# Linear attention and two MLPs on one core: query buffers, the place of an output split, and how the next pass's weights and first operands are fetched

## The chip, the core and the metric

The program runs on one NeuronCore of one Trainium2 chip. The core has a matrix engine (TensorE, shown as PE, with its weight loads as PEld), a vector engine (VectorE, DVE), an activation engine (ScalarE, ACT), a general engine (GpSimd, POOL) and a sequencer that here issues nearly all DMAs (SyncE, SP). Each engine executes its own instructions strictly in the order in which the program lists them, and waits at an instruction until the semaphores that it needs are set. The metric is the device time of one execution in microseconds (us); lower is better.

## What is computed

The reference, cut to what matters:

```python
kv  = np.einsum('bhsd,bhse->bhde', k, v)           # 8 batches, 8 heads, 576 tokens, 64 wide
o   = np.einsum('bhsd,bhde->bhse', q, kv)
rms = np.sqrt(np.mean(o * o, axis=-1, keepdims=True) + 1e-06)
x   = o / rms * g_norm                              # as 4608 tokens x 512
h   = x @ w_in                                      # 512 x 2048
x   = np.maximum(0.01 * h, h) @ w_out               # 2048 x 512
h   = np.maximum(x @ w_in2, 0.0)                    # the second MLP
out = (h * h) @ w_out2
```

## The kernel before

All products are made in pairs of reduced-width float32 operands: a value is split into a high part (ACT copies it, rounding) and a low part (the difference), and a product is three matmuls, high by high, high by low, low by high.

**Pass 1** makes x and the first product, h = x @ w_in, block by block: 9 blocks of 512 tokens, and in each block 16 slots (block j, slot m), a slot being 12 matmuls of 512 columns in `gemm1` (line 471). `leaky` (line 483, on ACT) takes the sum out of PSUM into one of four buffers `h`, and SP stores it to a scratch tensor `g` in DRAM. Of the eight PSUM banks, `gemm1` uses four in turn. The attention that makes block j+1's x is spread over block j's slots, in 8 units of 256 tokens by 2 heads; block 0's own attention stands ahead of everything ("attention 0"). A unit goes through these stages: `stage_a` transposes q (line 368) and splits it into `qh` (ACT) and `ql` (DVE); `stage_b` makes the output `ops` (lines 384 to 386), its square `sq` and its copy `osb` (ACT), and splits the square into `sqh` (DVE, line 394) and `sql` (POOL, line 395); `stage_s` sums over the head (`ssps`, lines 401 and 402); `stage_c` makes the norm (`y`, `z` on ACT at lines 410 and 411, three DVE instructions at lines 412, 415 and 418, the last of which writes `osb`); `stage_d` splits `osb` into `xh` (ACT, line 427) and `xl` (POOL, line 428). The sixteen pieces of w_in are rounded by `scale_w` (ACT line 173, DVE lines 174 and 177) and `join_w` (DVE lines 187 and 191) and split by `split_w` (ACT line 203, POOL line 204), three of them in attention 0 and the rest in block 0. From block 1 on the weights of the later passes are rounded, summed and split the same way, and their operands stored to DRAM as `w2_01`, `w2_10` and `w2_11`.

**Pass 2** (line 662, with `ph` 0) multiplies `g` by w_out in seven products per two-by-two group instead of eight: a group is 7 steps of 12 matmuls of 256 columns. Its weight operands are 28 slots `w2_01_0` to `w2_01_27` of 512 KB, loaded by `fetch` (line 281); its data operands are loaded from `g` by `load_g2` (line 515, two loads of 512 KB for a group), summed on DVE (`sum_op`, line 542) and split on ACT (`hi_op`, line 557) and DVE (`lo_op`, line 562). Passes 3 and 4 do the same for the second MLP.

**What sets the order.** The list `prog` is written out by small tables: stages are put at slots, and sorted inside one slot by the tuple `order`. Nothing reorders it later; each engine's order is that of the list. Loads of q, k, v and raw weights stand as early in SP's order as there are free buffers: a load of q is emitted when `stage_a` frees one of the `Q_BUFS` buffers, and waits on SP until PE has read that buffer. Large SBUF tiles come from 42 slots; `take_big` hands out the one that has been free longest. `fetch` loads the next wanted weight slot when the number of resident weights is under `cap`; in pass 1's last block `gemm1` gives back one of the 16 w_in pieces after each slot and calls `fetch` again. A store of `h` is emitted one slot after its `leaky`.

Of the kernel before, what the change touches and what calls it, by code (L numbers as in the profile page):

```python
# [18 lines left out]
def tile_linear_attention_two_mlps(  # L19
# [36 lines left out]
    NM = DFF // P  # L56
# [7 lines left out]
    EPS = 1e-6  # L64
    LD_BUFS, Q_BUFS, KV_BUFS = 8, 3, 6

# [643 lines left out]
    with tc.manual_schedule():  # L710
# [9 lines left out]
        for u in sorted(steps):  # L720
            order = ("d", "b", "a", "s", "c", "kv", "gn", "scale", "join", "w")
            prog += sorted(steps[u], key=lambda st: order.index(st[0]))
        prog.append(("mlp",))
        slots = [(j, m) for j in range(NB) for m in range(NM)]
        steps = {}

# [26 lines left out]
        for s, (j, m) in enumerate(slots):  # L753
            if m == 0 and j + 1 < NB:
                at0, pace = (s - 4, 2) if j else (s, 1.4)
                put(at0, "x", j + 1)
                lags = (2, 4, 5) if j else (1, 2, 3)
                for n, sts in attention_steps(j + 1, pace, 0, *lags).items():
                    for st in sts:
                        put(at0 + n, *st)  # L760
        put(NM * (NB - 1), "cap", 28)
        put(NM * (NB - 1), "want", (0, 1), 0, NSLOT)
        late = ("w", "join", "scale", "ws", "w2")
        for s in range(len(slots)):
            st = steps.pop(s, ())
            prog += [x for x in st if x[0] in late]
            if s:
                prog.append(("lk", *slots[s - 1]))
            prog.append(("g1", *slots[s]))
            order = ("d", "s", "c", "b", "a", "kv")  # L770
            prog += sorted((x for x in st if x[0] in order), key=lambda x: order.index(x[0]))
            prog += [x for x in st if x[0] not in order and x[0] not in late]
        prog.append(("lk", *slots[-1]))
        assert not steps


        ev = []
# [41 lines left out]
        for x, (half, z) in enumerate(insts):  # L819
# [5 lines left out]
            if not (x and insts[x - 1][1] == z):  # L825
                lead = 11 if x and len(SETS[insts[x - 1][1]]) == 1 else 15
                at_slot(t0 - lead - XLEAD, "xl", z)
                for y, (kind, name) in enumerate(prep("T")):
# [36 lines left out]
        second_pass(t3, 1, [j for half, z in insts if half for j in SETS[z]])  # L865
        prog += [st for t, st in sorted(ev, key=lambda e: e[0])]
        prog += [("tick",)] * 3
# [84 lines left out]
```

## Time and profile before

| | |
|---|---|
| median of 3 runs | 1698.28 us (1698.13 to 1699.26) |
| profiled execution, device time | 1698.46 us |
| span shown by its profile | 1696.6 us |
| TensorE busy, VectorE busy, ScalarE busy | 95%, 72%, 47% of the span |
| mean granted TensorE clock over the span | 0.984 |

The profiled execution is 0.18 us over the median of the timed runs, and its span is 1.9 us shorter than its device time. Times inside the profile count from the start of the span. Pass 1 runs from 0 to 588 us, pass 2 from 598 to about 960 us. In a timeline row the columns are the start in us, the duration in us, engine, line, operation, output<-inputs, shapes and count; the square bracket gives how long the engine stood idle before the row and what ended the wait.

### The profile page before, as it was taken

What the parts mean: (1) busy time and instruction counts of PE and PEld (TensorE: products, weight loads), DVE (VectorE), ACT (ScalarE), POOL (GpSimd) and SP (SyncE); (2) the same over time, 40 slices, a digit from 0 to 9 for tenths busy, and PEclk for the clock granted to TensorE, in tenths of its full rate; (3) what the DMA queues carried; (4) which work ended last, traced back from release to release, by engine and by line L of the source; (5) the groups of instructions that cost most, each with busy time, mean ns of one, the idle gap of its engine ahead of it and who ended that gap; (6) DMA issues with size and microseconds to landing.
All of it is one profiled execution on the core that took longest, in us unless ns stands there. A gap on an engine that the chain in (4) does not pass through costs nothing. (4 is left out here: it accounts for less than half of the span.)

```text
span 1696.6 us, 28822 instructions
## 1 busy us (share of the span) xinstructions
PE 1613.3 (95%) x10672; PEld 1453.6 (86%) x10672; DVE 1227.0 (72%) x2047; ACT 792.8 (47%) x1655; POOL 269.4 (16%) x344
## 2 busy tenths in 40 slices
PE   5889989989989789999999999999999899999999
PEld 3668778778877589999999988878887899999999
DVE  5876677767675078888787787756876588788886
ACT  4656657566665144343444444434544344444342
POOL 3444455454545000000000000000000000000000
PEclk9999999999999989999999999999999999999999
DMA  7757979989976934444444744485457944334342
GB/s 192 218 153 222 319 239 313 290 276 305 316 271 238 407 137 128 128 132 132 146 134 149 280 149 156 161 286 173 149 167 261 346 140 140 128 125 131 125 135 84
DMA packets 249452, 338.50 MB, mean 200 GB/s; under 512 B 55264, under 2 KB 180192, under 8 KB 249312
## 3 DMA queue, kind: packets, MB, share of 16 engines
q1 hardware_dynamic: 249152, 336.67, 60.4%
q8 instruction: 84, 1.38, 0.3%
q14 instruction: 56, 0.46, 0.1%
q10 hardware_dynamic: 160, 0.00, 0.0%
HBM read 198.18 MB, written 138.41 MB: 198 GB/s over the span
## 5 line engine op out<-in xcount | busy, mean ns | idle before, releaser
L471 PE MATMUL hps<-xh,w 128*128 128x512 f32 x1152 | 388.0, 407 | 15.7 <-ACT xh L427 9.1
L471 PEld LDWEIGHTS hps<-xh,w 128*128 128x128 f32 x1152 | 222.6, 194 | 69.0 <-ACT xh L427 12.5
L471 PE MATMUL hps<-xl,w 128*128 128x512 f32 x576 | 231.4, 402 | 10.0 <-POOL xl L428 10.0
L471 PEld LDWEIGHTS hps<-xl,w 128*128 128x128 f32 x576 | 112.0, 195 | 33.9 <-POOL xl L428 13.3
L483 ACT ACTIVATE h<-hps 128x512 f32<-128x512 f32 x144 | 85.2, 592 | 47.2 <-DMA g<-h 36.5
L577 DVE TENSOR_TENSOR h_C<-aps,u 128x512 f32<-128x512 f32 x72 | 49.5, 688 | 64.4 <-PE aps L598 32.5
L412 DVE SCALAR_TENSOR_TENSOR z<-ssps,z 128x256 f32<-128x256 f32 x72 | 30.3, 421 | 86.5 <-ACT z L411 86.1
L395 POOL TENSOR_TENSOR sql<-sq,sqh 128x256 fp32r<-128x256 f32 x72 | 53.3, 741 | 204.5 <-DVE sqh L394 185.8
L428 POOL TENSOR_TENSOR xl<-osb,xh 128x256 fp32r<-128x256 f32 x72 | 63.6, 883 | 18.3 <-ACT xh L427 18.2
L577 DVE TENSOR_TENSOR u<-bps,p 128x512 f32<-128x512 f32 x72 | 49.4, 687 | 20.9 <-PE bps L598 10.8
L191 DVE SCALAR_TENSOR_TENSOR wt<-wt,w_raw 128x512 uint32<-128x512 uint32 x64 | 58.7, 917 | 2.2
L174 DVE TENSOR_SCALAR w_raw<-w_raw 128x512 uint32<-128x512 uint32 x64 | 36.3, 567 | 30.0 <-ACT wt L173 29.9
L410 ACT ACTIVATE y<-ssps,eps 128x256 f32<-128x256 f32 x72 | 33.9, 471 | 51.4 <-PE ssps L402 51.2
L615 ACT ACTIVATE h_C<-aps 128x512 f32<-128x512 f32 x36 | 21.5, 598 | 77.1 <-issue 30.0
L598 PE MATMUL aps<-op_B21h,w 128*128 128x512 f32 (+1 forms) x160 | 52.2, 375 | 5.3 <-ACT p L608 5.3
L177 DVE SCALAR_TENSOR_TENSOR w_raw<-w_raw 128x512 uint32<-128x512 uint32 x64 | 55.6, 869 | 2.2
L598 PE MATMUL aps<-op_B22h,w 128*128 128x512 f32 (+1 forms) x160 | 52.0, 375 | 2.5 <-DVE h_C L577 2.5
L598 PE MATMUL bps<-op_T4h,w 128*128 128x512 f32 (+1 forms) x160 | 51.6, 371 | 2.2 <-DVE u L577 2.2
L598 PE MATMUL aps<-op_B11h,w 128*128 128x512 f32 (+1 forms) x160 | 51.2, 369 | 0.2 <-DVE h_C L577 0.2
L598 PE MATMUL bps<-op_T3h,w 128*128 128x512 f32 (+1 forms) x160 | 51.1, 369 | 0.0
L608 ACT ACTIVATE p<-aps 128x512 f32<-128x512 f32 x36 | 21.2, 589 | 64.0 <-PE aps L598 64.0
L598 PE MATMUL bps<-op_T2h,w 128*128 128x512 f32 (+1 forms) x160 | 51.0, 368 | 0.0
(1408 smaller groups left out, 4360.1 us busy)
## 6 DMA issues: line engine op xcount, KB each, us to landing
g_raw<-g SPq DMA_DIRECT2D x144, 512.0 KB, 4.6
w<-w SPq DMA_DIRECT2D x84, 512.0 KB, 7.6
g<-h SPq DMA_DIRECT2D x144, 256.0 KB, 4.8
g<-h_C SPq DMA_DIRECT2D x144, 256.0 KB, 2.4
w_raw<-in_moe_w_in_dram SPq DMA_DIRECT2D x32, 512.0 KB, 5.9
w_raw<-in_moe_w_out_dram SPq DMA_DIRECT2D x32, 512.0 KB, 5.9
w<-whS SPq DMA_DIRECT2D x64, 256.0 KB, 3.7
x_raw<-x SPq DMA_DIRECT2D x32, 512.0 KB, 6.1
```

The source lines that it names most:

```text
L174: nc.vector.tensor_scalar(out=upper, in0=upper, scalar1=0x80000000, scalar2=None, op0=ALU.bitwise_and)
L177: nc.vector.scalar_tensor_tensor(out=lower, in0=lower, scalar=29, in1=upper, op0=ALU.logical_shift_right, op1=ALU.bitwise_or,)
L191: nc.vector.scalar_tensor_tensor(out=t, in0=t, scalar=3, in1=lower, op0=ALU.logical_shift_left, op1=ALU.bitwise_or,)
L395: nc.gpsimd.tensor_tensor(out=sql, in0=sq, in1=f32(sqh), op=ALU.subtract)
L410: nc.scalar.activation(out=y, in_=ps, func=AF.Abs_reciprocal_sqrt, bias=eps)
L412: nc.vector.scalar_tensor_tensor(out=z, in0=ps, scalar=EPS, in1=z, op0=ALU.add, op1=ALU.mult)
L428: nc.gpsimd.tensor_tensor(out=xl[:, p % 2, c], in0=osb, in1=f32(xh[:, p % 2, c]), op=ALU.subtract)
L471: nc.tensor.matmul(out=ps, lhsT=w[:, wh, c * P:(c + 1) * P], rhs=x_t[j][xh, c // 2][0][:, c % 2, :], start=(c == 0 and y == 0), stop=(c == ...
L483: nc.scalar.activation(out=h, in_=h_ps.pop((j, m)), func=AF.Prelu, alpha=0.01)
L577: nc.vector.tensor_tensor(out=t, in0=x, in1=y, op=ALU.add)
L598: nc.tensor.matmul(out=ps[:, p], lhsT=w[:, wh, c, :], rhs=t[xh][:, c, :], start=(fresh and p == 0 and c == 0 and y == 0), stop=(p == len(p ...
L615: nc.scalar.activation(out=h, in_=ps, func=AF.Relu)
```

## The change

Five things change, and no arithmetic: the same instructions are executed with the same operands.

1. `Q_BUFS` goes from 3 to 6.
2. In the sort inside a step or a slot, `stage_d` ("d") comes behind the stages of the later units ("b", "a", "s", "c") instead of ahead of them.
3. The tiles of block j+1's x are taken at the start of block j instead of four slots before it.
4. Pass 2's weight slots are wanted from block 5 on and fetched under a rising cap (one more at block 5 slot 8, block 6 slots 2 and 12, block 7 slot 6 and block 8 slot 0, then more quickly), where before the cap was raised to 28 at the start of block 8 and all free room was filled at once.
5. What pass 2 does ahead of its first matmul (the loads, sums and splits of its first group) is put into pass 1's last six slots, two steps to a slot. The loads of the third pass's first x come 6 steps later than before.

```diff
-    LD_BUFS, Q_BUFS, KV_BUFS = 8, 3, 6
+    LD_BUFS, Q_BUFS, KV_BUFS = 8, 6, 6
...
-            order = ("d", "b", "a", "s", "c", "kv", "gn", "scale", "join", "w")
+            order = ("b", "a", "s", "c", "d", "kv", "gn", "scale", "join", "w")
...
+        CAPS = ((17, -40), (18, -30), (19, -20), (20, -10), (21, 0), (22, 3), (24, 5))
...
-                put(at0, "x", j + 1)
+                put(s, "x", j + 1)
...
-        put(NM * (NB - 1), "cap", 28)
-        put(NM * (NB - 1), "want", (0, 1), 0, NSLOT)
...
-            order = ("d", "s", "c", "b", "a", "kv")
...
+        put(NM * (NB - 4), "want", (0, 1), 0, NSLOT)
+        for n, at0 in CAPS:
+            put(NM * (NB - 1) + at0, "cap", n)
...
-                at_slot(t0 - lead - XLEAD, "xl", z)
+                at_slot(t0 - lead - XLEAD if x else t0 - 19, "xl", z)
...
-        prog += [st for t, st in sorted(ev, key=lambda e: e[0])]
+        ev.sort(key=lambda e: e[0])
+
+        for t, st in ev:
+            if t < 0:
+                put(len(slots) + t // 2, *st)
...
+            order = ("s", "c", "b", "a", "d", "kv")
...
+            if s == len(slots) - 1:
+                prog.append(("cap", 28))
...
+        prog += [st for t, st in ev if t >= 0]
```

In the built programs the order of PE's and DVE's instructions is the same before and after, from the first to the last; only buffer numbers differ. ACT's and POOL's orders differ in attention 0 and block 0, and ACT's again in the last four slots of block 8; between these they are the same. SP's order differs in more places. Three of them follow; the names hold block or unit numbers and a running number at their end.

At the start of the program, SP's DMA issues behind the last v of batch 0 stand before the change like this (q_raw1_0 is the q of unit 4 of attention 0):

```order
L149 DMA w_raw0_0_0_334<-in_moe_w_in_dram 128x4x256
L149 DMA w_raw0_1_0_336<-in_moe_w_in_dram 128x4x256
L357 DMA q_raw0_3_345<-in_q_dram 128x2x64 x2
L149 DMA w_raw0_2_0_363<-in_moe_w_in_dram 128x4x256
L149 DMA w_raw0_3_0_365<-in_moe_w_in_dram 128x4x256
L357 DMA q_raw1_0_389<-in_q_dram 128x2x64 x2
```

and with the change like this:

```order
L357 DMA q_raw0_3_299<-in_q_dram 128x2x64 x2
L357 DMA q_raw1_0_302<-in_q_dram 128x2x64 x2
L357 DMA q_raw1_1_305<-in_q_dram 128x2x64 x2
L149 DMA w_raw0_0_0_343<-in_moe_w_in_dram 128x4x256
L149 DMA w_raw0_1_0_345<-in_moe_w_in_dram 128x4x256
L357 DMA q_raw1_2_354<-in_q_dram 128x2x64 x2
```

Three units' q now stand ahead of the first two weights, and the weights three q later. From here on a q load stands where one stood before, but is that of a unit three further on.

In attention 0, ACT's instructions of one step stand before the change like this:

```order
L427 ACTIVATE xh0_1_317<-osb0_2_469 128x256
L392 ACTIVATE sq1_0_548<-ops1_0_544 128x256
L393 ACTIVATE osb1_0_549<-ops1_0_544 128x256
L371 ACTIVATE qh1_1_559<-qtps1_1_556 128x256
L410 ACTIVATE y0_3_570<-ssps0_3_567,eps_90 128x256
L411 ACTIVATE z0_3_571<-y0_3_570 128x256
L173 ACTIVATE wt0_1_0_577<-w_raw0_1_0_336 128x512
```

and with the change like this:

```order
L392 ACTIVATE sq1_0_558<-ops1_0_554 128x256
L393 ACTIVATE osb1_0_559<-ops1_0_554 128x256
L371 ACTIVATE qh1_1_569<-qtps1_1_566 128x256
L410 ACTIVATE y0_3_580<-ssps0_3_577,eps_90 128x256
L411 ACTIVATE z0_3_581<-y0_3_580 128x256
L427 ACTIVATE xh0_1_326<-osb0_2_477 128x256
L173 ACTIVATE wt0_1_0_589<-w_raw0_1_0_345 128x512
```

The split of unit 2 (`xh0_1<-osb0_2`), which needs DVE's last norm instruction of that unit, moved from the head of the step to behind the five instructions of units 3, 4 and 5.

At the start of block 8 of pass 1, SP's issues stand before the change like this (the piece shown begins behind eleven loads `w2_01_0` to `w2_01_10`, which follow each other):

```order
L281 DMA w2_01_11_6850<-w2_01_11_119 128x1024
L281 DMA w2_01_12_6852<-w2_01_12_120 128x1024
L237 DMA g0_7_3_223<-h7_15_6812 128x2x256
L281 DMA w2_01_13_6878<-w2_01_13_121 128x1024
L237 DMA w2_11_24_188<-whB22_11_6_6746 128x512
L237 DMA w2_11_25_189<-whB11_11_7_6859 128x512
L237 DMA g0_8_0_224<-h8_0_6862 128x2x256
```

and with the change like this, behind the store of h7_14:

```order
L281 DMA w2_01_4_6836<-w2_01_4_112 128x1024
L281 DMA w2_01_5_6838<-w2_01_5_113 128x1024
L237 DMA g0_7_3_223<-h7_15_6820 128x2x256
L281 DMA w2_01_6_6864<-w2_01_6_114 128x1024
L237 DMA w2_11_24_188<-whB22_11_6_6754 128x512
L237 DMA w2_11_25_189<-whB11_11_7_6845 128x512
L237 DMA g0_8_0_224<-h8_0_6848 128x2x256
```

Thirteen loads of 512 KB stood ahead of the store of block 7's last `h`, and two do now; the first four went into blocks 5 to 7. Later in the block the loads of pass 2's first group stand behind the store of h8_8 and `w2_01_18`, where before they stood behind the store of h8_14 and `w2_01_27`.

At the end of block 8, ACT's instructions stand before the change like this:

```order
L483 ACTIVATE h8_12_7099<-hps8_12_7084 128x512
L483 ACTIVATE h8_13_7117<-hps8_13_7102 128x512
L483 ACTIVATE h8_14_7135<-hps8_14_7120 128x512
L483 ACTIVATE h8_15_7153<-hps8_15_7138 128x512
L557 ACTIVATE op0_(0, 0)_T2_7168<-sT2_0_(0, 0)_7162 128x512
L557 ACTIVATE op0_(0, 0)_B11_7170<-g_raw0_0_0_0_7156 128x512
```

and with the change like this:

```order
L557 ACTIVATE op0_(0, 0)_T2_7103<-sT2_0_(0, 0)_7097 128x512
L557 ACTIVATE op0_(0, 0)_B11_7105<-g_raw0_0_0_0_7055 128x512
L483 ACTIVATE h8_12_7108<-hps8_12_7080 128x512
L557 ACTIVATE op0_(0, 0)_B21_7126<-g_raw0_0_0_1_7057 128x512
L557 ACTIVATE op0_(0, 0)_T3_7132<-sT3_0_(0, 0)_7129 128x512
L483 ACTIVATE h8_13_7134<-hps8_13_7111 128x512
L557 ACTIVATE op0_(0, 0)_T1_7152<-sT1_0_(0, 0)_7095 128x512
L557 ACTIVATE op0_(0, 0)_T4_7158<-sT4_0_(0, 0)_7156 128x512
L483 ACTIVATE h8_14_7160<-hps8_14_7137 128x512
```

The seven splits of pass 2's first group now stand between the last four `leaky`, the first two of them ahead of h8_12's.

## Rows read from the trace of the kernel before

**Rows 1.** Busy time by stretch: from:to, length, engines' busy us, clock, DMA

```profile
0.00:600.00 600.00, 534.68 (x2951) 434.17 (x2952) 391.77 (x784) 337.95 (x894) 269.41 (x344) 0.96 0.84 270
610.00:960.00 350.00, 350.00 (x2919) 350.00 (x2918) 278.84 (x444) 144.65 (x254) 0.00 (x0) 1.00 0.45 144
```

**Rows 2.** Waits of PE, whole program: total us, times, longest us

```profile
PE hps L471 <- POOL xl L428: 10.0, 7, 3.4
...
PE hps L471 <- ACT xh L427: 9.1, 5, 4.1
```

**Rows 3.** Timeline of PE in attention 0

```profile
20.81 0.70 PE L368 MATMUL qtps<-ident,q_raw 128*128 128x128 f32 x2 [3.05 <-DMA q_raw<-in_q_dram]
...
24.62 0.76 PE L368 MATMUL qtps<-ident,q_raw 128*128 128x128 f32 x2 [1.38 <-DMA q_raw<-in_q_dram]
...
49.16 0.79 PE L471 MATMUL hps<-xh,w 128*128 128x512 f32 x1 [0.51 <-ACT xh L427]
```

**Rows 4.** Timeline of SP at the start: DMA issues

```profile
12.53 1.00 SPq L149 DMA_DIRECT2D w_raw<-in_moe_w_in_dram  x2
13.65 0.95 SPq L357 DMA_DIRECT2D q_raw<-in_q_dram  x2
```

**Rows 5.** Instructions on w_raw, 12.5 to 25 us: its five DMAs

```profile
DMA to landing us min/median/max: 4.1/7.4/8.2
```

**Rows 6.** Timeline of DVE in attention 0

```profile
21.97 0.42 DVE L372 TENSOR_TENSOR ql<-qtps,qh 128x256 fp32r<-128x256 f32 x1 [2.55 <-ACT qh L371]
23.00 0.42 DVE L412 SCALAR_TENSOR_TENSOR z<-ssps,z 128x256 f32<-128x256 f32 x1 [0.60 <-ACT z L411]
...
24.32 0.42 DVE L174 TENSOR_SCALAR w_raw<-w_raw 128x512 uint32<-128x512 uint32 x1
...
31.70 1.50 DVE L174 TENSOR_SCALAR w_raw<-w_raw 128x512 uint32<-128x512 uint32 x1
...
47.17 0.42 DVE L412 SCALAR_TENSOR_TENSOR z<-ssps,z 128x256 f32<-128x256 f32 x1 [1.30 <-ACT z L411]
```

**Rows 7.** Timeline of POOL in attention 0

```profile
31.52 1.40 POOL L204 TENSOR_TENSOR w<-wt,w 128x512 fp32r<-128x512 f32 x1 [0.64 <-ACT w L203]
```

**Rows 8.** Timeline of ACT in attention 0

```profile
24.43 0.42 ACT L427 ACTIVATE xh<-osb 128x256 fp32r<-128x256 f32 x1 [0.92 <-DVE osb L418]
```

**Rows 9.** Busy time by stretch, block 8 and after, columns as in rows 1

```profile
560.00:570.00 10.00, 9.49 (x34) 7.40 (x35) 0.00 (x0) 1.65 (x3) 0.00 (x0) 0.83 1.05 405
570.00:580.00 10.00, 9.25 (x41) 7.33 (x40) 0.00 (x0) 2.99 (x5) 0.00 (x0) 1.00 1.05 407
...
598.00:604.00 6.00, 5.82 (x29) 5.52 (x30) 5.19 (x9) 3.33 (x6) 0.00 (x0) 0.59 0.39 147
```

**Rows 10.** Timeline of PE, block 8 and the start of pass 2

```profile
538.03 0.77 PE L471 MATMUL hps<-xl,w 128*128 128x512 f32 x1 [1.64 <-POOL xl L428]
...
560.51 0.50 PE L471 MATMUL hps<-xh,w 128*128 128x512 f32 x1 [3.79 <-ACT h L483]
...
571.56 0.50 PE L471 MATMUL hps<-xh,w 128*128 128x512 f32 x1 [0.75 <-ACT h L483]
...
587.81 0.39 PE L471 MATMUL hps<-xh,w 128*128 128x512 f32 x1
598.04 2.37 PE L662 MATMUL ps<-op_(0, 0)_T,w 128*128 128x256 f32 x7 [9.84 <-ACT op_(0, 0)_T L557]
```

**Rows 11.** Timeline of ACT, block 8 and the start of pass 2

```profile
559.86 0.60 ACT L483 ACTIVATE h<-hps 128x512 f32<-128x512 f32 x1 [13.34 <-DMA g<-h]
...
597.36 0.63 ACT L557 ACTIVATE op_(0, 0)_T<-sT_(0, 0)_7162 128x512 fp32r<-128x512 f32 x1 [8.47 <-DVE sT_(0, 0)_7162 L542]
```

**Rows 12.** Timeline of DVE at the start of pass 2

```profile
595.31 0.69 DVE L542 TENSOR_TENSOR sT_(0, 0)_7160<-g_raw 128x512 f32<-128x512 f32 x1 [52.61 <-DMA g_raw<-g]
```

**Rows 13.** DMA issues, 538 to 600 us: size, median us from issue to landing

```profile
w<-w SPq DMA_DIRECT2D x28, 512.0 KB, 7.7
g<-h SPq DMA_DIRECT2D x18, 256.0 KB, 7.0
```

More of the change, by code (lines that the diff above doesn't have):

```diff
@@ L760, in tile_linear_attention_two_mlps @@
                         put(at0 + n, *st)
-        put(NM * (NB - 1), "cap", 28)
-        put(NM * (NB - 1), "want", (0, 1), 0, NSLOT)
[L763 to L769, printed above, removed]
-            order = ("d", "s", "c", "b", "a", "kv")
[L771 to L774, printed above, removed]
+        put(NM * (NB - 4), "want", (0, 1), 0, NSLOT)
+        for n, at0 in CAPS:
+            put(NM * (NB - 1) + at0, "cap", n)
         ev = []
@@ L865, in tile_linear_attention_two_mlps @@
         second_pass(t3, 1, [j for half, z in insts if half for j in SETS[z]])
-        prog += [st for t, st in sorted(ev, key=lambda e: e[0])]
+        ev.sort(key=lambda e: e[0])
+        for t, st in ev:
+            if t < 0:
+                put(len(slots) + t // 2, *st)
+        late = ("w", "join", "scale", "ws", "w2")
+        for s in range(len(slots)):
+            st = steps.pop(s, ())
+            prog += [x for x in st if x[0] in late]
+            if s:
+                prog.append(("lk", *slots[s - 1]))
+            prog.append(("g1", *slots[s]))
+            order = ("s", "c", "b", "a", "d", "kv")
+            prog += sorted((x for x in st if x[0] in order), key=lambda x: order.index(x[0]))
+            prog += [x for x in st if x[0] not in order and x[0] not in late]
+            if s == len(slots) - 1:
+                prog.append(("cap", 28))
+        prog.append(("lk", *slots[-1]))
+        assert not steps
+        prog += [st for t, st in ev if t >= 0]
         prog += [("tick",)] * 3
```

## Prediction, made before the changed kernel ran

> **What bounds the kernel now.** I read the stretches first. In pass 2 TensorE never stops: 350.00 of 350 us busy at full clock. In pass 1 it is busy 534.68 of 600 us and its clock was 0.96 on average [rows 1]. So what a change can win lies in the first 600 us, where 65 us are idle and some more are lost to the low clock, and there only at places where PE itself waits. The view of PE's waits says that the two largest are for the splits `xl` and `xh` of line 427 and 428, 19.1 us together [rows 2]. Most of these stand where one block of pass 1 follows another, and in the built programs every compute engine's order there, from block 1 on, is unchanged. I leave them as they are.
>
> Two other places are touched. The first is attention 0, where PE waits 3.05 and 1.38 us for a q that is still in flight [rows 3]. Its load was issued at 13.65, behind two loads of 512 KB [rows 4], and PE starts on it at 20.81, seven us later. But PE is not the bound there. DVE stands idle for 2.55 and 0.60 us when that q is late, and from 23 us to 47.17 almost never again [rows 6]: what sets the end of attention 0 is the sum of DVE's work behind those two gaps.
>
> The second is block 8 and the start of pass 2. PE waits 3.79 and 0.75 us for a `leaky` on ACT, and 9.84 us for pass 2's first split operand [rows 10]. ACT's `leaky` had itself waited 13.34 us for the store of an earlier `h` [rows 11], since four buffers hold them; and the DMA engines were full, at 405 to 407 GB/s and a share of 1.05 [rows 9]. The 28 loads of pass 2's weights are all in this stretch, and a store took 7.0 us to land, at the median [rows 13]. The first split of pass 2 waited for DVE, 8.47 us [rows 11], and DVE for the group's data, until 595.31 [rows 12]: those loads stand in SP's order behind all 28.
>
> **Six query buffers and the moved split: 3.7 us.** The q of units 3, 4 and 5 is issued ahead of the weights: three loads of some 1.0 us of issue each (0.95 for one [rows 4]), so the first weight goes out about 3 us later, at 15.6. The five weight loads there took 4.1 to 8.2 us [rows 5], so it lands between 19.7 and 23.8; they were slow because they stood behind each other, and the first had nothing of its size ahead of it, so I take an estimate near the low end, 20 us. Its first use in the new order is behind the first moved split, at about 20.7 by the same chain. So the weights are not late; and q, issued at 12.53 and smaller than a weight, should land before 12.53 + 4.1 = 16.6. DVE then has no reason for the gaps of 2.55 and 0.60: 3.15 us earlier for all that follows. The split of unit 6 no longer stands ahead of unit 7's norm on ACT; each such split made ACT wait for DVE's last norm instruction, 0.92 us in the first case shown [rows 8]. Where DVE is full this gives nothing, apart from the end: the last gap of 1.30 [rows 6] shortens, the last `xh` comes earlier, and PE's wait of 0.51 for it [rows 3] goes. 3.15 + 0.51 = 3.66. Bounds: nothing, if other work of DVE fills the gaps; 5.0 (2.55 + 0.60 + 1.30 + 0.51) if DVE's later gap goes too. I take 3.7, since the gaps are DVE's own and nothing is left ahead of q. In block 0 the same split moves behind five or fewer instructions; DVE has no idle time there to be won, so I take nothing. Cover: block 0 starts earlier by those 3.7 us, and so do the reads of PE that free q buffers, on which SP waits, so the loads behind them shift by the same.
>
> **x tiles four slots later: nothing.** The first write to them is five slots behind the old place, one behind the new. It only leaves four more SBUF slots free for longer.
>
> **Weights one by one: 6.2 us.** Four of the 28 loads leave block 8 and the first burst is cut up. A load takes 0.524 MB / 407 GB/s = 1.29 us of the DMA engines, a store of 256 KB 0.64 us. In block 8 stand now 20 loads up to its last slot (25.8 us), four loads of the first group (5.2), 15 stores of `h` (9.6) and 7 of weight operands (4.5): 45 us. PE needs for six slots, from 571.56 to the end of the row at 587.81 [rows 10], 16.4 us, so 2.74 for one and 43.8 for 16, and the wait of 1.64 at the block's start with its slow clock comes on top, some 47 in all. So the DMA engines keep up, but hardly. Slot by slot, I find the largest backlog in slot 5, where three loads come at once, at about 5 us; a store then lands about 7.5 us after its issue. A buffer of `h` is needed again after four slots, 10.9 us, so ACT does not wait, and PE has three banks, 8.2 us, behind that. The waits of 3.79 and 0.75 go, and with them the low clock behind the first (granted 0.83 over 560 to 570 [rows 9], 1.7 us lost): 6.2 us. Bounds: nothing, if the stores are as late as now; 6.2. I take the upper end, because the row of 13.34 us was a store that stood behind 13 loads, and now stands behind two. The four loads in blocks 5 to 7 cost the DMA engines 1.29 us each among other transfers; on SP each waits only for a tile that was given back at least three slots earlier, 8 us, by my count of the list of free tiles.
>
> The Trainium skill ("DMA: Bandwidth & Descriptors", section "Where 436 GB/s comes from") names a limit of about 358 GB/s of HBM for one core. By that the 45 us would be 51, more than PE's 47, and the stores would set the pace of block 8 again. The trace disagrees for a core alone: 407 GB/s over 10 us [rows 9].
>
> **First group in pass 1: 12.3 us.** Its two loads stand behind the store of h8_8, which is ready nearly seven slots before the end of the block, some 17 us; with a backlog of 4 us, two loads of 1.29 and 2 us to land they are there 9 us before the end. DVE's first two sums (0.69 [rows 12], twice) and ACT's split (0.63 [rows 11]) and DVE's low part come to 2.7 us. So PE finds the first operand ready when its last slot ends, and the wait of 9.84 goes. The clock behind it, 0.59 over 598 to 604 [rows 9], lost 2.46 us; PE no longer stops, so that goes too: 12.3. Cost: four `leaky` of ACT now stand behind splits that wait for that data. The first, h8_12, would be due 7.5 us before the end and comes some 4 us before it; the bank is needed again in pass 2's fifth step. DVE is idle there (52.61 us in one wait [rows 12]), so its order costs nothing. If the group were late by L beyond its 6 us of cover, PE would wait L again. Bounds: 0 to 12.3; I take all of it.
>
> **The later x loads of pass 3: nothing.** Issued four steps ahead of their first sum instead of ten, they have some 6 us, against 7.7 for the slowest such median [rows 13]; DVE is eight steps ahead there.
>
> **Sum.** 3.7 + 6.2 + 12.3 = 22.2 us. The profiled execution took 1698.46 us, 0.18 over the median of the runs: 1698.46 - 22.2 = 1676.3 us.
>
> **Rivals.**
> 1. *Attention 0 gives nothing.* Rows for: the same DVE instruction took 0.42 us alone and 1.50 beside POOL's 1.40 [rows 6, 7], and the moved split brings its POOL half next to DVE's norm instructions; two or three of them stretched by 1.08 us eat the gain. Against: as many POOL instructions overlapped others before. 1698.5 - 18.5 = 1680.0. The Trainium skill ("GPSIMD Engine Reference", section "1. Specifications") gives the mechanism, SBUF interfaces shared with VectorE; the trace agrees with it, 0.42 against 1.50.
> 2. *Block 8 stays bound by transfers.* The 45 us of transfers against some 47 leave little room; if the stores are late again the 6.2 stay: 1676.3 + 6.2 = 1682.5. The limit that the Trainium skill names under "DMA: Bandwidth & Descriptors" belongs to this case.
> 3. *The first group is late.* If its data come 15 us after where I put them, PE waits as before: 1676.3 + 12.3 = 1688.6. For it: loads of this group took 8 us and more from issue behind a full queue. Against: 17 us of lead.
> 4. *Slower.* A fetch in blocks 5 to 7 whose tile is still read holds SP, and with it the stores of `h`. The trace's hold of 13.34 us [rows 11] cost PE 3.79 + 0.75 and 1.7 of clock, 6.2 us. Four such holds cost 24.8: 1676.3 + 24.8 = 1701. It decides from 5.6 us a hold. Against: the tiles were freed slots ahead.
> 5. *No effect:* what is won is waited for at the next block boundary, as where PE waits for `xl`, since POOL and DVE are unchanged there: 1698.
>
> **How the numbers follow.** The forecast 0.58, its own range 1672 to 1680; rival 1 0.15, rival 2 0.11, rival 3 0.08, rival 4 0.03, rival 5 0.05. From 1670 (the forecast with 1.3 us more in attention 0 and a block boundary or two that fall better) to 1685 (rivals 1 and 2, or both in part) lies 0.83. A measurement of this kernel can tell about 0.2%, 3.4 us: faster 0.93, same 0.04, slower 0.03.
>
> **What would show it.** PE's timeline: no wait of 3 us for q near 20; the row now at 49.16 some 4 us earlier and without a wait; no wait of line 471 for `h` in block 8; line 662 starting within 1 us of the last row of line 471; no low clock behind. ACT: no wait of `h` for DMA over 2 us in block 8. I am wrong if waits for `xl` and `xh` at the block boundaries grow, if DVE between 20 and 112 us is busy for longer than before, or if a fetch in blocks 5 to 7 holds SP.

## The result, and the profile after

The changed kernel takes 1670.49 us, the median of 4 runs (1669.91 to 1672.58), against 1698.20 (1697.62 to 1699.26) for the kernel before: ratio 0.9838, 95% interval 0.9821 to 0.9855, so 27.7 us faster. The forecast was 1676.3 with a range of 1670 to 1685: the sign and the places were right, the size was 5.8 us short, and the time lies 0.5 us inside the range's low end and 1.5 us outside the forecast's own range of 1672 to 1680.

The profiled execution has a span of 1668.1 us against 1696.6, a gain of 28.5. The busy time by stretch, with the columns of [rows 1], and under it the two rows of PE's waits over the whole program that answer to [rows 2]:

```profile
0.00:570.00 570.00, 519.13 (x2939) 424.10 (x2940) 388.52 (x780) 333.11 (x886) 268.87 (x344) 0.97 0.85 271
580.00:930.00 350.00, 349.29 (x2909) 348.88 (x2909) 280.42 (x446) 145.85 (x257) 0.00 (x0) 1.00 0.46 153
```

```profile
PE hps L471 <- ACT xh L427: 10.5, 5, 4.0
PE hps L471 <- POOL xl L428: 10.2, 7, 3.1
```

Pass 1 is over near 571 and no longer near 588. The waits for `xh` and `xl` at the block starts are 20.7 us, and were 19.1 (with 0.51 inside block 0): nothing was won there, and blocks 1 to 7 took no longer for it (410.71 us against 410.70, in the table below).

In attention 0, on the timelines of SP, PE and DVE (they answer to [rows 3, 4, 6]):

```profile
12.53 3.02 SPq L357 DMA_DIRECT2D q_raw<-in_q_dram  x6
15.59 1.02 SPq L149 DMA_DIRECT2D w_raw<-in_moe_w_in_dram  x2
```

```profile
17.23 0.63 PE L368 MATMUL qtps<-ident,q_raw 128*128 128x128 f32 x2
...
19.57 0.63 PE L368 MATMUL qtps<-ident,q_raw 128*128 128x128 f32 x2
...
40.17 0.63 PE L471 MATMUL hps<-xh,w 128*128 128x512 f32 x1
```

```profile
18.49 0.42 DVE L372 TENSOR_TENSOR ql<-qtps,qh 128x256 fp32r<-128x256 f32 x1
19.32 0.42 DVE L412 SCALAR_TENSOR_TENSOR z<-ssps,z 128x256 f32<-128x256 f32 x1 [0.41 <-ACT z L411]
...
27.87 1.49 DVE L174 TENSOR_SCALAR w_raw<-w_raw 128x512 uint32<-128x512 uint32 x1
...
41.44 0.42 DVE L412 SCALAR_TENSOR_TENSOR z<-ssps,z 128x256 f32<-128x256 f32 x1 [0.54 <-ACT z L411]
```

Three query loads go out together ahead of the first weight, which leaves at 15.6 as forecast. The two `qtps` rows that waited for a q, at 20.81 and 24.62, start at 17.23 and 19.57 without a wait. The same rows of DVE as in [rows 6] show the gap of 2.55 gone, that of 0.60 at 0.41 and that of 1.30 at 0.54. The first row of block 0's matmuls, at 44.61 before, stands at 40.17: 4.4 us earlier. The row that stood at 49.16 behind a wait starts at 44.02 without one.

Block 8 and the start of pass 2: the stretches, the DMA issues of 525 to 575, and the timelines of ACT, DVE and PE (for [rows 9 to 13]):

```profile
550.00:560.00 10.00, 10.00 (x46) 8.28 (x45) 0.00 (x0) 2.12 (x4) 0.00 (x0) 1.00 1.04 409
560.00:570.00 10.00, 10.00 (x46) 8.29 (x45) 1.38 (x2) 1.48 (x3) 0.00 (x0) 1.00 1.05 411
570.00:576.00 6.00, 6.00 (x46) 5.54 (x45) 4.48 (x7) 4.17 (x8) 0.00 (x0) 1.00 1.05 412
```

```profile
w<-w SPq DMA_DIRECT2D x21, 512.0 KB, 7.6
g<-h SPq DMA_DIRECT2D x18, 256.0 KB, 7.2
g_raw<-g SPq DMA_DIRECT2D x4, 512.0 KB, 8.6
```

```profile
551.35 0.60 ACT L483 ACTIVATE h<-hps 128x512 f32<-128x512 f32 x1 [5.03 <-DMA g<-h]
...
570.03 0.63 ACT L557 ACTIVATE op_(0, 0)_T<-sT_(0, 0)_7097 128x512 fp32r<-128x512 f32 x1 [5.54 <-DVE sT_(0, 0)_7097 L542]
```

```profile
568.07 0.69 DVE L542 TENSOR_TENSOR sT_(0, 0)_7095<-g_raw 128x512 f32<-128x512 f32 x1 [33.57 <-DMA g_raw<-g]
```

```profile
570.99 0.39 PE L471 MATMUL hps<-xh,w 128*128 128x512 f32 x1
571.21 0.97 PE L662 MATMUL ps<-op_(0, 0)_T,w 128*128 128x256 f32 x5
...
592.11 0.39 PE L662 MATMUL ps<-op_(0, 2)_T,w 128*128 128x256 f32 x1 [0.37 <-ACT op_(0, 2)_T L557]
592.83 1.45 PE L662 MATMUL ps<-op_(0, 2)_T,w 128*128 128x256 f32 x10 [0.34 <-DVE op_(0, 2)_T L562]
```

From 550 to 576 PE is busy without a break at the full clock. The DMA engines are as full as before, and ACT still waits for a store, 5.03 us at the longest; PE's banks hide it now. The first of the group's data let DVE start only 2.9 us ahead of the last row of pass 1, and the first row of pass 2 follows that row by 0.22 us.

By stage, from the starts of the first and last rows of line 471 in each block, of line 662 and of line 598, in the profiled execution of every kernel that was run (us; "pass 2 wait" is from the last row of line 471 to the first of line 662):

| kernel | attention 0 | block 0 | blocks 1-7 | block 8 | pass 2 wait | pass 2 | rest |
|---|---|---|---|---|---|---|---|
| before | 44.61 | 78.25 | 410.70 | 54.25 | 10.23 | 365.40 | 733.22 |
| after | 40.17 | 74.47 | 410.71 | 45.63 | 0.23 | 364.30 | 732.62 |
| q6 | 41.17 | 75.20 | 410.25 | 53.91 | 10.23 | 365.23 | 733.85 |
| split | 45.03 | 77.31 | 408.91 | 55.09 | 10.27 | 364.88 | 733.63 |
| q6_split | 41.23 | 76.08 | 413.66 | 53.94 | 10.22 | 365.65 | 734.41 |
| q6_split0 | 41.02 | 74.16 | 413.40 | 54.43 | 10.23 | 365.45 | 733.34 |
| q_second | 45.24 | 77.81 | 408.76 | 55.13 | 10.27 | 364.80 | 733.17 |
| x_alone | 43.91 | 79.07 | 409.72 | 54.41 | 10.26 | 365.30 | 733.29 |
| fetch | 44.30 | 76.69 | 414.37 | 45.63 | 14.62 | 365.53 | 733.01 |
| group | 45.32 | 78.28 | 411.15 | 54.17 | 0.23 | 363.54 | 732.09 |
| after_burst | 40.30 | 76.09 | 410.81 | 54.00 | 0.23 | 363.40 | 735.16 |
| after_nogroup | 40.93 | 74.51 | 410.10 | 45.63 | 14.93 | 365.40 | 736.31 |
| after_warm | 46.69 | 74.69 | 413.52 | 45.63 | 0.23 | 363.60 | 733.86 |
| after_early | 40.66 | 76.60 | 402.71 | 43.29 | 1.25 | 364.32 | 734.01 |

Some columns repeat closely: block 8 is 45.63 in four kernels, the wait 0.23 in four. Others scatter where an edit does little or nothing: blocks 1 to 7 from 408.8 to 414.4, leaving out the last row. One profile is therefore no measure of an edit worth 2 us; the medians and intervals below are. Differences given as ratios are turned into time with the 1698 to 1700 us of the kernel before.

### The profile page after: what moved, and what is told of

Read it like the earlier page. It is cut to its first block, busy times and chain, and to the rows that moved or that the text cites. A ratio compares the mean times of both kernels' runs of the same rounds, so it can differ in the third digit from the quotient of the medians.

```text
span 1668.1 us, 28839 instructions
## 1 busy us (share of the span) xinstructions
PE 1598.6 (96%) x10672; PEld 1444.0 (87%) x10672; DVE 1225.8 (73%) x2047; ACT 791.5 (47%) x1655; POOL 268.9 (16%) x344
## 5 line engine op out<-in xcount | busy, mean ns | idle before, releaser
L471 PE MATMUL hps<-xh,w 128*128 128x512 f32 x1152 | 381.1, 401 | 16.0 <-ACT xh L427 10.5
L471 PEld LDWEIGHTS hps<-xh,w 128*128 128x128 f32 x1152 | 218.9, 190 | 66.8 <-ACT xh L427 13.7
L471 PE MATMUL hps<-xl,w 128*128 128x512 f32 x576 | 228.0, 396 | 10.2 <-POOL xl L428 10.2
L615 ACT ACTIVATE h_C<-aps 128x512 f32<-128x512 f32 x36 | 21.6, 599 | 77.9 <-issue 29.8
```

The lines of the kernel that those rows point to most:

```text
L471: nc.tensor.matmul(out=ps, lhsT=w[:, wh, c * P:(c + 1) * P], rhs=x_t[j][xh, c // 2][0][:, c % 2, :], start=(c == 0 and y == 0), stop=(c == ...
```

## The experiments

### Which query edit, and where block 0's time went

q6 is the kernel before with this alone:

```diff
-    LD_BUFS, Q_BUFS, KV_BUFS = 8, 3, 6
+    LD_BUFS, Q_BUFS, KV_BUFS = 8, 6, 6
```

> The kernel before with six query buffers and nothing else. Theory A (the q waits are what held attention 0, the split's place costs little): DVE's 2.55 and 0.60 us gaps near 22 and 23 go, attention 0 ends about 3 us earlier, and part of what block 0 gave follows: 1691 to 1695 us. Rival B (the split that stands first holds the rows behind it as soon as q no longer does): under 1.5 us, 1697 us or more.

Measured: 1695.95 us (10 runs, 1691.64 to 1700.11), ratio 0.9990, interval 0.9979 to 1.0001. In the trace attention 0 ends 3.4 us earlier and block 0 is 3.1 us shorter, as theory A has it, but the traced execution is the fastest of the ten (1691.64), and the median is 1695.95, 1 us above the band of theory A and 1 us below that of B. The q waits are gone (the same row of `qtps` starts at 20.13 without a wait); what the whole run keeps of it is not resolved from nothing.

split is the kernel before with the sort keys alone, in both places:

```diff
-            order = ("d", "b", "a", "s", "c", "kv", "gn", "scale", "join", "w")
+            order = ("b", "a", "s", "c", "d", "kv", "gn", "scale", "join", "w")
...
-            order = ("d", "s", "c", "b", "a", "kv")
+            order = ("s", "c", "b", "a", "d", "kv")
```

> The kernel before with the split sorted behind the other stages, in attention 0 and in pass 1's loop, with three query buffers. Theory A: the q waits stay, only the 0.51 us wait and what block 0 gains by the loop's order can come, 1696 to 1698 us. Rival B (the split's place is the main part of the 8.2 us that attention 0 and block 0 gave together): 1690 to 1693 us.

Measured: 1696.29 us (11 runs), ratio 0.9990, interval 0.9981 to 0.9998: within theory A's band. The timeline of DVE in attention 0 shows why it does not do more; the q waits stay, and a second one appears, where the kernel before had no gap:

```profile
21.37 0.42 DVE L372 TENSOR_TENSOR ql<-qtps,qh 128x256 fp32r<-128x256 f32 x1 [3.03 <-ACT qh L371]
...
26.69 0.42 DVE L372 TENSOR_TENSOR ql<-qtps,qh 128x256 fp32r<-128x256 f32 x1 [1.16 <-ACT qh L371]
```

q6_split makes both edits.

> Six query buffers and the split behind, both places, nothing of the fetch, of the x tiles or of the first group. If the 8.2 us by which block 1 starts earlier in the changed kernel comes of these two edits: 1690 us (1689 to 1691), first matmul of block 0 at 40.2, of block 1 at 114.7. If the x tiles or the fetch have a share in it: 1692 to 1694 us, with the difference in block 0.

Measured: 1693.03 us (7 runs), ratio 0.9971, interval 0.9960 to 0.9981: 4.9 us faster, 3.2 to 6.8. The forecast's term was 3.7. In its trace, of the slowest of the seven executions (1697.01), block 1 starts 5.5 us earlier than before, not 8.2, and blocks 1 to 7 are 3 us longer.

q6_split0 has six buffers and moves the split in attention 0 alone (the first of the two sort keys above).

> Six query buffers and the split behind in attention 0 alone; pass 1's loop sorts it first as before. Theory C (block 0's 3.8 us are what attention 0's earlier end brings with it, by a TensorE at the full clock from block 0's start): as the run with both places, 1690 us, block 0 lasting 74.5 us. Rival D (the loop's order gave them, by ACT's xh copies no longer standing ahead of the next units' rows in block 0): 1693.5 to 1694.5 us, block 0 lasting 78 us as before.

Measured: 1692.60 us (5 runs), ratio 0.9962, interval 0.9948 to 0.9976; block 0 lasts 74.16. That speaks for theory C against D: the loop's order is not what shortens block 0. In the traces a shorter block 0 goes with six buffers. The medians say less: six buffers alone are worth 1.7 us (-0.2 to 3.6), with the moved split in attention 0 6.5 (4.1 to 8.8), so what the split adds to the buffers may be several us, and no trace shows where. Over all traces, block 0 lasts 76.7 to 79.1 in the six with three buffers for attention 0 (mean 77.9) and 74.2 to 76.6 in the eight with six (mean 75.2), and without the kernel that adds matmuls, attention 0 ends at 44.7 and 40.8 in the mean. What differs inside block 0 is shown by the same two rows, PE's last wait there for a `w` of GpSimd, of the kernel before and of q6, each with the 10 us that begin some 5.8 us ahead of the row, in the columns of [rows 1]. The kernel before:

```profile
107.72 1.00 PE L471 MATMUL hps<-xh,w 128*128 128x512 f32 x2 [0.83 <-POOL w L204]
```

```profile
102.00:112.00 10.00, 7.54 (x25) 5.13 (x23) 9.72 (x15) 4.96 (x10) 6.06 (x6) 0.83 0.11 38
```

And q6:

```profile
102.81 0.73 PE L471 MATMUL hps<-xh,w 128*128 128x512 f32 x2 [0.84 <-POOL w L204]
```

```profile
97.00:107.00 10.00, 7.53 (x49) 5.37 (x48) 9.72 (x16) 5.42 (x14) 6.06 (x6) 1.00 0.14 44
```

The same row after the same wait, and PE was busy as long in each stretch: behind the first, part of it is granted the low level, 1.2 of 2.4 GHz, behind the second none. From that row to block 1 it is 15.14 us (122.86 - 107.72) in the one and 13.55 (116.36 - 102.81) in the other, 1.6 of the 3.1 us. The kernel before has another such dip, a granted clock of 0.91 over 80 to 100, where q6 has 1.00.

q_second keeps three buffers for attention 0 and gives all later attention three of its own:

```diff
-        a = qp.tile([P, 2, P], F32, tag="q", name=f"q_raw{i}_{p}")
+        own = {"tag": "q", "bufs": 3} if i < TB // U else {"tag": "q2", "bufs": 3}
+        a = qp.tile([P, 2, P], F32, name=f"q_raw{i}_{p}", **own)
```

> The kernel before with three q buffers for attention 0 and three others for all later attention, nothing else. With six shared buffers block 0 lasted 75.2 us against 78.3. Theory G (block 0 is shorter since SyncE's q load no longer stands 13.5 us ahead of block 0's other loads): attention 0 ends as before at 44.6 us (44 to 45.5), block 0 lasts 75 to 76 us. Theory C (block 0 is shorter since attention 0 hands over earlier, and a TensorE at its full clock): block 0 stays at 77 to 78.5 us, the time within 1 us of before.

Measured: 1698.25 us (12 runs), ratio 0.9998, interval 0.9988 to 1.0008; attention 0 45.24, block 0 77.81. Theory G falls: block 0's own q loads are not what it waits for, and free buffers there bring nothing. Attention 0 has to have them.

The other half of theory C, a TensorE at its full clock from block 0's start, is contradicted by the traces of the kernel before and of the changed one, around the start of block 0 (44.61 and 40.17). Before:

```profile
24.00:44.00 20.00, 10.26 (x31) 7.17 (x31) 19.11 (x36) 12.85 (x34) 11.65 (x12) 1.00 0.50 132
```

After:

```profile
24.00:44.00 20.00, 11.12 (x31) 7.97 (x31) 17.73 (x33) 12.62 (x32) 12.29 (x14) 0.50 0.62 158
```

The kernel before enters block 0 at the full level and takes 78.25 us for it; the changed kernel enters it at the low level and takes 74.47.

after_warm asks after the same part of theory C with an edit. It adds work on constants, in PE's idle time of attention 0, which the next matmul overwrites:

```diff
+        for _ in range(12 if i < TB // U else 0):
+            nc.tensor.matmul(out=ps[:, :P], lhsT=ones, rhs=ones, start=True, stop=True)
         nc.tensor.matmul(out=ps, lhsT=ones, rhs=sqh, start=True, stop=False)
```

> The changed kernel with twelve more 128-column matmuls ahead of each of attention 0's sum-of-squares matmuls, on constants and overwritten by the real one, to keep TensorE busier in its waits there. Theory C (the clock at attention 0's end and block 0's start is worth some us): the granted clock between 24 and 44 us, 0.57 to 0.67 in the changed kernel's profile, rises to over 0.9 and block 1 starts 1 to 2.5 us earlier, 1668 to 1670 us. Rival (attention 0 waits for VectorE, ACT and GpSimd alone, and the added matmuls stand in front of real ones): block 1 starts 0 to 2 us later, 1670 to 1673 us.

Measured: 1680.74 us (4 runs), ratio to before 0.9897, interval 0.9884 to 0.9910, some 10 us slower than the changed kernel. The stretches of its trace around the start of block 0, at 46.69:

```profile
30.00:46.00 16.00, 14.62 (x68) 14.13 (x67) 13.29 (x24) 10.00 (x25) 7.60 (x10) 0.50 0.56 145
46.00:54.00 8.00, 7.98 (x43) 5.86 (x43) 4.86 (x11) 3.60 (x9) 3.60 (x4) 0.68 0.05 12
```

The clock did not rise: it is 0.50 here, and the changed kernel too was granted 0.50 from 24 to 44, not the 0.57 to 0.67 of the expectation. The added rows delay attention 0 by 6.5 us, so the expectation failed for the clock and the rival was too mild; the rest of the 10 us lies in stages that the edit does not touch. Block 0 begins here at the low level and 6.5 us late, and still lasts 74.69, so a start at the low level does not by itself make it long. But with TensorE late, VectorE and ACT may have been further ahead at that start; what the handover is worth is not settled by this run.

x_alone is the edit of the x tiles, on the kernel before:

```diff
-                put(at0, "x", j + 1)
+                put(s, "x", j + 1)
```

> The kernel before with the next block's x tiles taken at the block's first slot and not four slots ahead, nothing else. If the edit is only what the spread fetch needs to find buffers, as forecast: no change, 1697 to 1700 us, blocks 1 to 7 as long as before to within 1 us each. Rival (the tiles are late for the first splits, which now stand right behind): TensorE's waits for xh and xl at the block starts grow by 0.3 to 1 us each, 1701 to 1705 us.

Measured: 1696.78 us (11 runs), ratio 0.9999, interval 0.9988 to 1.0010: nothing, as forecast.

### The fetch and the first group, one without the other

fetch is the kernel before with the x tiles' edit, the `CAPS` table, the list wanted from block 5 and the cap of 28 at the last slot. (By the list of free tiles the spread fetch cannot do without the x tiles' edit: buffers run out.)

```diff
-        put(NM * (NB - 1), "cap", 28)
-        put(NM * (NB - 1), "want", (0, 1), 0, NSLOT)
+        put(NM * (NB - 4), "want", (0, 1), 0, NSLOT)
+        for n, at0 in CAPS:
+            put(NM * (NB - 1) + at0, "cap", n)
```

> The kernel before with the spread fetch (from block 5, the caps) and the x tiles taken at the block's first slot, without which its buffers run out; no first group in pass 1, no query edits. Theory E (block 8 was held by the burst, and pass 2's start by loads that stand behind pass 1's end): block 8 shorter by 6 to 8.6 us, the 9.84 us wait at pass 2's start shrinks by at most 2: 1687.5 to 1692 us. Rival F (the burst caused the late first group as well): the wait goes to 3 us or less, 1680 to 1684 us.

Measured: 1695.65 us (11 runs), ratio 0.9976, interval 0.9967 to 0.9985, so 4.1 us faster, less than either theory. Block 8 is 8.6 us shorter, as theory E has it; but the wait in front of pass 2 grows by 4.4. The rows, of DVE, of PE and of the stretches:

```profile
592.89 0.69 DVE L542 TENSOR_TENSOR sT_(0, 0)_7160<-g_raw 128x512 f32<-128x512 f32 x1 [48.38 <-DMA g_raw<-g]
```

```profile
580.99 0.39 PE L471 MATMUL hps<-xh,w 128*128 128x512 f32 x1
595.62 1.74 PE L662 MATMUL ps<-op_(0, 0)_T,w 128*128 128x256 f32 x4 [14.24 <-ACT op_(0, 0)_T L557]
```

```profile
581.00:598.00 17.00, 2.62 (x10) 1.95 (x9) 3.79 (x6) 2.74 (x5) 0.00 (x0) 0.58 1.03 411
```

Pass 1 ends 6.8 us earlier than in [rows 10], the group's data only 2.4 us earlier than in [rows 12], since they stand behind the remaining weights and the engines move 411 GB/s without a pause. What the compute engines gained, the transfers could not follow.

group is the opposite: the kernel before, with its burst, and the events of t < 0 put into pass 1's last slots (the last hunk of the diff, the later `xl` too).

> The kernel before with the first group's loads, sums and splits in pass 1's last slots, the fetch in one burst at block 8 as before. Theory E (two separate causes): the wait at pass 2's start goes, less what the loads lose behind the burst: 1688 to 1692 us. Rival F (the burst keeps the group's loads and holds VectorE and ACT in block 8 while they wait): 1696 us or more, with new waits in block 8.

Measured: 1686.23 us (5 runs), ratio 0.9924, interval 0.9911 to 0.9936: 12.9 us faster, 1.8 us beyond theory E's band; F is out. The wait at pass 2's start is gone, block 8 as long as before (its largest wait of PE for `h` is 4.93 us, 3.79 before), and pass 2 1.9 us shorter.

after_burst is the changed kernel with the first two lines of the last diff in place of the rest.

> The changed kernel with the burst fetch of before (cap 28 and the whole list at block 8's first slot), all else as changed. Theory E: block 8's 8.6 us come back, pass 2's start stays without a wait of more than 2 us: 1678 to 1680 us. Rival F (the first group needs the spread fetch to be there in time): 1686 to 1690 us.

Measured: 1680.74 us (4 runs), ratio 0.9891, interval 0.9876 to 0.9907: as expected, to within 1 us. Block 8 is 54.00 again, and the two waits of [rows 10] are back nearly to the digit:

```profile
554.08 0.50 PE L471 MATMUL hps<-xh,w 128*128 128x512 f32 x1 [3.81 <-ACT h L483]
...
564.97 0.50 PE L471 MATMUL hps<-xh,w 128*128 128x512 f32 x1 [0.78 <-ACT h L483]
```

after_nogroup is the changed kernel with the events of t < 0 behind pass 1's last row.

> The changed kernel with all of pass 2's first group behind pass 1's last row, as before; query edits and spread fetch stay. Theory E: 8 to 10 us of wait at pass 2's start come back and some of it again as low clock behind: 1679 to 1682 us. Rival F: at most 3 us come back, 1671 to 1674 us.

Measured: 1690.54 us (5 runs), ratio 0.9949, interval 0.9937 to 0.9962. That is 20 us over the changed kernel (19 by the ratios), where theory E expected 9 to 12: the wait is 14.93 and not 10.23, pass 2 is 1.1 us longer, and another 3.7 us of the traced execution lie in passes 3 and 4, which the edit does not touch. The four corners, as differences of the ratio times 1699 us: from the kernel with the query edits alone (-4.9) the fetch brings another 3.7, the group 13.6 (after_burst, -18.5), both 22.6 (-27.5). The two are worth about 5 us more together than apart, a difference of four intervals that are 1.8 to 2.9 us wide on either side, so about as uncertain as it is large; the table is the better witness: without the group in pass 1, a shorter block 8 is followed by a wait that is 4.4 to 4.7 us longer.

### A step further

after_early changes one number of the changed kernel, so that the last split of the next block's x stands two slots ahead of that block's start:

```diff
-                at0, pace = (s - 4, 2) if j else (s, 1.4)
+                at0, pace = (s - 4, 1.8) if j else (s, 1.4)
```

> The changed kernel with attention's units in blocks 1 to 7 spread over 1.8 slots each and not 2, so that the last split of the next block's x stands two slots ahead of that block's first matmul and not in the slot just ahead. TensorE's waits for xh and xl at the starts of blocks 2 to 8 are 20.7 us together in the changed kernel's profile (2.64, 0.56, 0.99, 3.13, 0.93, 4.04, 0.28, 1.09, 0.73, 1.75, 2.90, 1.65). Theory H (they come only of the split's late place): they go but for 2 to 6 us: 1652 to 1658 us. Rival I (VectorE's and ACT's rows of attention and weight sums are as dense, and the waits move into the block): 1666 to 1671 us.

Measured: 1664.70 us (5 runs, 1662.16 to 1665.50), ratio to before 0.9794, interval 0.9781 to 0.9807, clear of the changed kernel's 0.9821 to 0.9855. It is faster than both kernels, between the two theories. The waits of PE in its blocks 1 to 8 (117 to 563), where the changed kernel has 20.7 us for `xh` and `xl`:

```profile
PE ssps L402 <- POOL sql L395: 4.9, 12, 0.6
PE ops L385 <- DVE ql L372: 3.6, 5, 1.5
PE ssps L401 <- DVE sqh L394: 2.4, 4, 1.1
PE ops L384 <- ACT qh L371: 2.2, 2, 1.6
```

The waits for `xh` and `xl` are gone altogether; 13.1 us of smaller ones stand in attention's own chain (the changed kernel had 1.9 of them in its blocks), since the units are closer to each other. The stages say what is left of it: blocks 1 to 8 are 10.3 us shorter, pass 2's first operands come 1.0 us late, and block 0, which the edit does not touch, was 2.1 longer in this execution.

## Why the prediction came out as it did

**Attention 0: right, and sized a little low.** The forecast was 3.15 for DVE's gaps and 0.51 for the late `xh`. At the first row of block 0 the trace shows 4.4, at the row of 49.16, where the forecast counts, 5.1, just over the upper bound of 5.0. The q waits carry it: from 14.4 us to the last `sqh` ahead of that first row DVE stands idle for 2.7 us, against 5.8, which is the forecast's 3.15 within 0.1. The other 1.3 are rows of DVE that took less time, which the forecast did not have. Six buffers alone end attention 0 3.4 us earlier, the moved split alone ends it no earlier. Rival 1's stretch did come, at the norm: line 418 takes 0.75 to 0.83 us in six of eight rows, and took 0.48 in six of eight before. But line 394 no longer takes up to 0.82 (0.28 to 0.32 now), and line 174 still takes 1.49 at its longest, as the 1.50 of [rows 6]; the same 51 rows come to 26.9 us and were 28.4. So the overlaps with POOL moved, and their sum fell.

**Block 0: the step that was mis-sized.** "In block 0 the same split moves behind five or fewer instructions; DVE has no idle time there to be won, so I take nothing." The trace of after shows 3.8 us, the means over the traces 2.7. (As medians of whole runs the two query edits are worth 4.9 us, against 3.7 taken, so not all that stands at block 1's start is kept.) For the split the traces bear the reasoning out (q6 has the shorter block without it); what it left out is the clock. DVE is full, but behind some of PE's short waits inside the block the granted clock fell in the kernel before, and the rows behind one such dip took 1.6 us longer than the same rows of q6. Taken over the whole block, as its length times the missing part of the mean granted clock (idle time counted in), the low level comes to 3.4 to 5.1 us in the six traces with three buffers (mean 3.9) and 0 to 3.3 in the eight with six (mean 1.3), while PE stood idle no less (9.0 and 9.8 us in the mean). So in the mean the clock is nearly all of the 2.7; in single traces it is not the whole account, as after_early, without any dip, lasts 76.60. Why six buffers make the dips rarer is open. It is not the q loads of block 0 (q_second), nor the clock at which the block begins; whether it is the earlier handover stays open, since after_warm moved more than the clock.

**x tiles: right**, nothing (x_alone).

**Weights one by one: mechanism right, 6.2 taken, 8.6 measured** (54.25 to 45.63). The waits of 3.79 and 0.75 and the low clock behind them went, as forecast. Of the 2.4 us left, 1.7 are, between these two traces, a low stretch at block 8's start that the forecast left on the bill of both kernels. The block's first 12 us, before and after:

```profile
533.00:545.00 12.00, 10.24 (x38) 7.75 (x37) 9.13 (x15) 5.78 (x15) 7.53 (x10) 0.86 0.98 330
```

```profile
525.00:537.00 12.00, 10.23 (x45) 7.91 (x44) 9.13 (x15) 5.77 (x15) 7.54 (x10) 1.00 0.97 327
```

PE is busy as long, and gets 45 matmuls done instead of 38: 0.14 of 12 us is 1.7 us of work, though the wait of 1.64 in front of it [rows 10] is still 1.65. This part is not the fetch's merit as such: four kernels with the burst (split, q_second, group, q6) have no low stretch there either, and last 53.9 to 55.1 us all the same, with a later wait for `h` of 4.9 to 5.9 us instead of 3.79. That speaks for the burst's late stores as what sets the length of block 8 there, wherever the time shows. The forecast's count of PE's own work in the block holds: 43.8 us for 16 slots and the wait of 1.65 make 45.4, against 45.63 measured. "ACT does not wait" was wrong: it waited 5.03 us, as stores took 7.2 us; the banks covered it. Rival 2 is out as to time, and not by much. The limit of about 358 GB/s for one core in the Trainium skill ("DMA: Bandwidth & Descriptors", section "Where 436 GB/s comes from") did not bind this lone core, which moved 409 to 412 GB/s from 550 to 576.

**First group: 9.84 of wait taken, 10.0 measured; 2.46 of clock taken, 1.1 measured.** The wait went in every kernel that has the edit. But "there 9 us before the end" was optimistic: DVE had the first data 2.9 us before the end, so the cover of 6 us was all used. The first split ended at 570.66, half a microsecond ahead of the row that needs it. The landing took what was forecast (4 + 2 x 1.29 + 2 us; the four loads' median is 8.6); the issue was late, 11.4 us before the end and not 17. SP's timeline, its issues:

```profile
557.04 0.32 SPq L281 DMA_DIRECT2D w<-w  x1
558.39 0.37 SPq L237 DMA_DIRECT2D g<-h  x1
559.02 0.32 SPq L281 DMA_DIRECT2D w<-w  x1
559.59 1.60 SPq L515 DMA_DIRECT2D g_raw<-g  x2
```

SP gives out one transfer at a time here, 0.6 to 1.4 us apart, about what a store and a load take of the DMA engines (0.64 and 1.29 in the forecast's reckoning); the section on the hardware says what holds it. The low clock behind the wait is gone (granted 1.00 over 571 to 605), but pass 2 is only 1.1 us shorter, in the kernels with the group and the burst 1.9 to 2.0 (365.4 to 363.5 and 363.4). The third group's operands came late, by 0.37 and 0.34 us; the other two kernels have one such wait, of 0.34 and 0.27, so the waits explain 0.4 of the difference and the rest is open. Rival 3 did not come, by a margin of half a microsecond.

**What the sum missed** is that the fetch and the group are not independent terms. Alone they are worth 4.1 and 12.9 us, together 22.6 on top of the query edits, where 18.5 was taken. Of these 22.6 the touched stages show 19.7 in the traces (8.3, 10.0 and 1.4 between q6_split and after); the other 3 us are in no stage that either edit touches, and whether they are scatter or a consequence is open. So the range was kept by 0.5 us and with some luck: block 0, block 8 and these 3 us were all sized too low, and little was too high but 1.3 us of clock in pass 2.

**Rivals 4 and 5.** No fetch in blocks 5 to 7 held SP: the four loads were issued at 390.75, 425.86, 464.98 and 496.98, each within 0.6 us of the end of the issue before it. Blocks 1 to 7 together took 410.71 us against 410.70, so nothing was given back in the trace of after. In those of q6_split and q6_split0 these blocks are 3 us longer, but PE is idle there no longer than before (19.4 and 19.1 us against 19.1); by the same count as for block 0, the low clock comes to 15.4 us in them and 11.9 in the kernel before. It comes to 15.4 in fetch too, without any query edit, so this is scatter of the clock and no wait at the block boundaries.

**A reading of the prediction to set right.** The 19.1 us of [rows 2] are not PE's two largest waits: the 9.84 us at pass 2's start stand between the two sums. The forecast prices that wait by itself, so its sum is unchanged.

## What to carry to other kernels

Where one queue feeds two stages at the full rate of the transfer engines, price its edits together: shortening the first stage alone moved half of its gain into a longer wait at the second, and only loads issued earlier turned it into time. Where an edit has two halves, run each alone, and read both the trace and the median: here the traces say that the buffers shortened attention 0 and the reordering beside them did not, while the medians of the whole program credit the buffers alone with less than the two together. After the edit, read what margin is left (2.9 us for the group's first data, none for the third group): the next gain or loss stands there.

## What the runs showed of the hardware

Equal waits of TensorE had unequal sequels. At the same row behind 0.83 and 0.84 us the granted clock was low once and full once, though TensorE had been busy for the same 3.5 of 6 us around that wait. At block 8's start a wait of 1.64 to 1.66 us stands in 13 of the 14 traces; the first 12 to 13 us of the block were granted 0.86 in five of them and 1.00 in eight. So in these pairs a short wait costs its own length or up to 1.7 us more, and which of these is not read from the wait.

Nor does the busy time in these rows tell it: between 24 and 44 us TensorE was granted 1.00 with 10.26 of 20 us busy in the kernel before and 0.50 with 11.12 in the changed one. Busy for 14.62 of 16 us on small matmuls in after_warm it was granted 0.50 all that time, and full speed came only in the stretch after. Filling idle time with work on constants raised nothing there and delayed attention 0 by 6.5 us.

An instruction of VectorE that ran beside one of GpSimd took up to three times as long (in attention 0, line 174: 0.42 alone and 1.50 us; line 394: 0.28 and 0.82), and with the splits moved other instructions were stretched.

SP never had more than eight transfers in flight, at any of its 1140 issues in the traces of before, after and fetch. Counted over each issue of SP with its landing, the number is eight at 51 of 55 issues between 540 and 600 us of the kernel before, at 34 of 51 between 530 and 580 of the changed one, at all 31 from 560 to 600 of fetch, and never nine. With eight in flight the next issue follows a landing at once: in the changed kernel 554.49, 557.04 and 559.02 behind landings at 554.43, 556.98 and 558.96. So behind a full queue a load is late twice, by its landing of some 8 us and by an issue that can't be made ahead, and a store behind it on SP with it. The prediction reckoned with the first alone.
